# A first unit set up in another order: u loaded between r and w, mask rows in another tile, r turned in other banks, a warm-up that multiplies a tile of ones

## The chip, the cores and the metric

The kernel runs on one core of one Trainium2 chip. Its time is the device time of one execution in microseconds (us); each kernel is run several times, and the median is given. A profile is taken of one further execution, with the start and the duration of every instruction of the five engines: TensorE (PE; its weight loads are PEld), VectorE (DVE), ScalarE (ACT), GpSimd (POOL) and SyncE (SP, which here only issues DMAs).

## The reference

A linear attention with a decaying state (rwkv6) is followed by a feed-forward layer with SiLU. All inputs are float32; B, H, S, D are 4, 8, 768, 48.

```python
state = zeros((B, H, D, D))
for t in range(S):
    cur = einsum('bhd,bhe->bhde', u[None] * k[:, :, t], v[:, :, t])
    y[:, :, t] = einsum('bhd,bhde->bhe', r[:, :, t], state + cur)
    state = w[:, :, t, :, None] * state + einsum('bhd,bhe->bhde', k[:, :, t], v[:, :, t])
x = y.transpose(0, 2, 1, 3).reshape(B * S, H * D)      # 3072 x 384
h = x @ w_in                                           # 384 x 2048
out = (h * (1 / (1 + exp(-h)))) @ w_out                # 2048 x 384
```

The term with u, here called the bonus, is what a token gives to itself: the sum over d of r * u * k, times v.

## The kernel before, in words

The work is cut into 12 units: 128 tokens of two of the four batch entries, all eight heads. A unit's scores (token against token, with the product of the decays between them) are built level by level: at level l, blocks of 2^l tokens are joined in pairs. For that the keys of the odd blocks are multiplied by products of the decays (`grow_keys`, L646 on GpSimd) and the queries by others (`grow_queries`, L628 on VectorE), TensorE multiplies them (`score_products`, L704 and L712), and masked copies take the new part over into `score` (`keep_masked`, L722). `start_keys` (L670) is the first step on the keys: two instructions with `own` true, two with `own` false, each over a quarter of the tokens, all with the decays of the odd tokens. `odd_ones` (L660, ScalarE) copies the keys that need no product at level 0 into the rows from which level 1 reads. `product` (L414) makes the pairwise products of the decays for the next level.

The order of every engine's queue is written out by hand: a call records its instructions in the order in which it stands, each engine takes its own in order, and a framework adds the semaphore waits. What follows concerns only the first unit's start.

- **Loads.** `load_tokens(0)` (L114) issues k, r and w as two halves each, one on SP's queue and one on ScalarE's. SP then issues u, spread over the 128 partitions (L281), the first piece of the weight `w_in` (L211), the tokens of unit 1 and further weights.
- **Set-up.** VectorE clears small tiles (L264 to L269). GpSimd makes the identity `ident`, writes rows of token numbers with iota (L330) into the first part of `score`, from which VectorE compares out the masks (L341, L344), and clears `score` when the last mask is made (L346); it then clears `block_sums` (L465).
- **Warm-up.** `beat(n)` (L1374) issues n transposes of `ident` into a PSUM bank that nobody reads. The first `beat`, of 16, stands ahead of the first turn; smaller ones (3, 5, 6, 2, 2) stand between later steps of unit 0.
- **Turns.** `turn(0, b, name)` brings a half of k, r or w, tokens on partitions, into the layout with features on partitions: eight matmuls against `ident` (`turn_in`, L377) into one of the two banks `p_m`, taken alternately, then copies by ScalarE (`turn_out`, L385 and L386 for k, L389 for r and w). The two banks `p_sc` are used later, for scores.
- **Bonus.** `bonus(0, x)` multiplies r and k, token by token and with the neighbour (x = 0 on GpSimd, L440; x = 1 on VectorE, L442), and then by u (x = 2, VectorE, L444). `bonus_sum` adds over the features (L449, L453), `bonus_spread` brings the sums to their tokens with four matmuls (L586), and `bonus_part` writes them into `score` (L602).
- **Order.** The call of `do` at L1384 sets unit 0's sequence up to level 1. In it `odd_ones` stands behind the turns of k, ahead of the turns of r. `bonus(0, 2)`, the product with u, stands behind the first sum and the turns of w.

Of the kernel before, what the change touches and what calls it, by code (L numbers as in the profile page):

```python
# [8 lines left out]
F32 = mybir.dt.float32  # L9
# [29 lines left out]
def kernel(  # L39
# [63 lines left out]
    def twos(room):  # L103

        flat = room.rearrange("p b h d -> p (b h d)")
        return flat[:, 0:H * 2 * D].rearrange("p (h s) -> p h s", h=H), flat[:, H * 2 * D:H * 2 * D + PD - D]
# [7 lines left out]
    def load_tokens(i):  # L114
        for name, src in (("k", k), ("r", r), ("w", w)):
            load_twos(twos(raw[:, i % NSLOT, WRK[name]])[0], src, i, [nc.sync, nc.scalar if i == 0 else nc.sync])
# [144 lines left out]

    load_tokens(0)
    zero = const.tile([128, 1], F32, name="zero")
# [8 lines left out]
    u_bc = const.tile([128, H, D], F32, name="u_bc")  # L272

# [7 lines left out]
    nc.sync.dma_start(out=u_bc, in_=u.partition_broadcast(128))  # L281
# [44 lines left out]
    for l in range(NL):  # L326
        c, ni = 1 << l, L >> (l + 1)

        first[l] = score[:, 0, 0].rearrange("p q t -> p (q t)")[:, l * 64:(l + 1) * 64].rearrange("p (i c) -> p i c", c=c)
        nc.gpsimd.iota(first[l], pattern=[[2 * c, ni], [0, c]], base=0, channel_multiplier=0,  # L330
                       allow_small_or_imprecise_dtypes=True)
        if l > 0:
            if l < NL - 2:
                masks[l] = const.tile([128, NB, ni, c], I8, name=f"mask{l}")
            else:
                masks[l] = late_masks[:, l - NL + 2].rearrange("p b (i c) -> p b i c", c=c)
# [33 lines left out]
    def turn_in(i, s, name):  # L370

        flat = raw[:, i % NSLOT, WRK[name]].rearrange("p b h d -> p (b h d)")
        p_tr = bank("p_m", NP, NB, L // 2)
# [17 lines left out]
    def clear_rest():  # L391

        for i in range(NSLOT):
            nc.gpsimd.memset(raw[:, i].rearrange("p x b h d -> p x (b h d)")[:, :, H * 2 * D + PD - D:], 0.0)
# [70 lines left out]
    nc.gpsimd.memset(block_sums, 0.0)  # L465
# [908 lines left out]
    def beat(n):  # L1374

        p = bank("p_m", L)
        for x in range(n):
            nc.tensor.transpose(p, ident, ident)

    def back(fn, i, *args):  # L1380
# [3 lines left out]
    do((make_spread,), (beat, 16), *both(turn, 0, "k"), (odd_ones, 0), (bonus, 0, 0), (bonus, 0, 1), *both(turn, 0, "r"),  # L1384
       (bonus_sum, 0, 0), (clear_state,), (clear_rest,), *back(turn, 0, "w"), (bonus, 0, 2), (bonus_sum, 0, 1), (start_keys, 0, nc.vector, True),
# [108 lines left out]
```

## Time and profile before

| What | us |
|---|---|
| median of 3 runs | 566.85 |
| lowest, highest | 566.71, 567.15 |
| the profiled execution's own time | 567.41 |
| its span, from first to last instruction | 565.6 |
| VectorE, GpSimd busy | 477.0, 395.7 |
| ScalarE busy | 274.5 |

Rows of the first 15 us, from the timeline (start, length):

| Row | us |
|---|---|
| `ident` ready on GpSimd (masks.py:199) | 1.01, 0.29 |
| `score` cleared by GpSimd (L346) | 5.64, 1.80 |
| product of r and k on VectorE (L442), after a wait for r's transfer | 7.11, 0.96 |
| neighbour product on GpSimd (L440) | 7.56, 1.38 |
| first sum on VectorE (L449) | 8.97, 0.55 |
| product with u on VectorE (L444) | 9.44, 0.95 |
| copies of w on ScalarE (L389) | 10.95, 0.64 and 11.82, 0.64 |
| start_keys on VectorE (L670, four) | 11.62, 1.31 |

How to read it: the chain of work that ended last is followed back from the last instruction, at each step to what released it, or to the instruction before it on its engine. Times count from the first instruction of the span. A matmul's duration covers its way through the array, and the next begins before it has ended, so starts, not durations, give the pace. Shares of busy time are averages over the whole span, and the part that is changed here is its first fortieth.

### The profile page before, as it was taken

Reading aid. Unit: us, or ns where it says so; the run is one execution under the profiler, and the core shown is the slowest. Engines: PE = TensorE matmul, PEld = TensorE weight load, DVE = VectorE, ACT = ScalarE, POOL = GpSimd, SP = SyncE. Lnnn points to the kernel's source line nnn. Section 1 sums busy time; section 2 is a strip of 40 time slices with the busy share of each in tenths; the row PEclk is TensorE's granted clock in tenths of the full one; section 3 lists DMA queues with packets and bytes.
Section 4 is the critical chain, followed back from the end, with each engine's and each line's share of the span. In section 5 each row is a group of like instructions: output and inputs, shape, how many; then the busy total and the mean of one; then the engine's idle time right before and its main releaser. Section 6 shows DMA issues by size and latency. Waiting matters only on the chain.

```text
span 565.6 us, 18886 instructions
## 1 busy us (share of the span) xinstructions
PE 555.8 (98%) x7782; PEld 517.6 (92%) x7782; DVE 477.0 (84%) x744; ACT 274.5 (49%) x620; POOL 395.7 (70%) x447
## 2 busy tenths in 40 slices
PE   8989999999999999999999999999999999999997
PEld 8767786699889999999999999999999999999997
DVE  7979788998999989999889989989989989882250
ACT  5679696362371373373374274274274272371330
POOL 5998988617879998969796696696696696700000
PEclk9999999999999999999999999999999999999999
DMA  9956876345345365365565554555555462102000
GB/s 224 314 104 191 213 213 133 49 69 115 99 76 99 80 105 94 59 131 95 104 104 93 113 93 89 108 96 94 111 88 95 99 102 65 38 5 57 29 9 21
DMA packets 206485, 57.59 MB, mean 102 GB/s; under 512 B 186048, under 2 KB 198208, under 8 KB 206400
## 3 DMA queue, kind: packets, MB, share of 16 engines
q1 hardware_dynamic: 203712, 54.23, 46.9%
q10 hardware_dynamic: 2688, 2.16, 1.6%
q8 instruction: 61, 1.00, 0.8%
q14 instruction: 24, 0.20, 0.1%
HBM read 47.14 MB, written 9.18 MB: 100 GB/s over the span
## 4 chain that ended last, share of the span: by engine, by line
PE 78%; DVE 8%; POOL 7%; DMA 3%; issue 2%; ACT 1%; SPq 0%; POOLq 0%; DVEq 0%
PE p_o L1335 24%; PE p_o L1191 14%; PE p_h L1191 9%; PE p_h L1084 8%; PE p_h L1335 4%; PE p_m L1273 4%; PE p_sc L704 3%; PE p_m L868 2%; PE p_sc L1335 2%; POOL tk L646 2%; POOL w_in_sb L260 2%; PE p_m L847 1%; DVE tr L628 1%; PE p_m L704 1%; POOL tw L414 1%
## 5 line engine op out<-in xcount | busy, mean ns | idle before, releaser
L646 POOL TENSOR_TENSOR tk<-tk,tw 128x256 f32<-128x256 f32 x112 | 91.7, 839 | 7.6 <-DVE tw L414 3.4
L1335 PE MATMUL p_o<-own,temps 128*128 128x192 f32 x496 | 82.9, 326 | 0.0
L1335 PEld LDWEIGHTS p_o<-own,temps 128*128 128x128 f32 x496 | 80.8, 190 | 0.3 <-DVE temps L1306 0.2
L1191 PE MATMUL p_o<-xt,w_in_sb 128*64 128x128 f32 x1152 | 72.5, 273 | 0.1
L414 POOL TENSOR_TENSOR tw<-tw 128x256 f32<-128x256 f32 (+6 forms) x71 | 42.3, 596 | 38.0 <-DVE tw L365 34.5
L1084 PE MATMUL p_h<-xt,w_in_sb 128*128 128x256 f32 x288 | 66.1, 384 | 1.8 <-POOL w_in_sb L260 1.6
L1191 PEld LDWEIGHTS p_o<-xt,w_in_sb 128*64 128x64 f32 x1152 | 64.9, 137 | 0.4 <-issue 0.4
L1084 PEld LDWEIGHTS p_h<-xt,w_in_sb 128*128 128x128 f32 x288 | 53.6, 190 | 10.0 <-POOL w_in_sb L260 2.4
L497 POOL TENSOR_TENSOR ruk<-tokens_rk 128x384 f32<-128x384 f32 x48 | 53.6, 1137 | 8.1 <-DMA tokens_rk<-in_k_dram 8.1
L1335 PE MATMUL p_o<-w_out_sb,gt 128*128 128x192 f32 x308 | 54.5, 330 | 0.4 <-DVE ob L1343 0.3
L628 DVE TENSOR_TENSOR tr<-tr,tw 128x512 f32<-128x512 f32 x57 | 51.9, 911 | 1.0 <-PE p_m L704 0.4
L1335 PEld LDWEIGHTS p_o<-w_out_sb,gt 128*128 128x128 f32 x308 | 50.0, 190 | 1.5 <-DVE ob L1343 0.9
L655 POOL TENSOR_TENSOR tk<-tk,tw 128x256 f32<-128x256 f32 x32 | 25.1, 812 | 27.5 <-DVE tk L365 27.5
L1306 DVE TENSOR_TENSOR temps<-gt 128x512 f32<-128x512 f32 (+1 forms) x48 | 42.9, 931 | 0.0
L1340 ACT COPY partial<-p_o 128x192 f32<-128x192 f32 x31 | 9.9, 319 | 66.6 <-PE p_o L1335 61.5
L616 ACT COPY tk<-tk 128x256 f32<-128x256 f32 x52 | 20.9, 402 | 37.2 <-POOL tk L646 27.4
L1215 ACT ACTIVATE gt<-p_o 128x512 f32<-128x512 f32 x45 | 26.0, 601 | 25.0 <-PE p_o L1191 25.0
L1335 PE MATMUL p_o<-w_out_sb,temps 128*128 128x192 f32 x176 | 30.5, 326 | 0.0
L722 DVE COPY_PREDICATED score<-mask,p_sc 128x512 f32<-128x512 int8 x38 | 28.4, 807 | 1.4 <-PE p_sc L704 1.3
L1335 PE MATMUL p_h<-w_out_sb,gt 128*128 128x192 f32 x168 | 29.1, 326 | 0.0
L1335 PEld LDWEIGHTS p_o<-w_out_sb,temps 128*128 128x128 f32 x176 | 28.9, 190 | 0.1
L497 POOL TENSOR_TENSOR spare<-tokens_rk 128x384 f32<-128x384 f32 x24 | 28.5, 1198 | 0.6
(251 smaller groups left out, 1314.0 us busy)
## 6 DMA issues: line engine op xcount, KB each, us to landing
w_out_sb<-in_moe_w_in_dram SPq DMA_DIRECT2D x6, 768.0 KB, 7.4
turned<-yt SPq DMA_DIRECT2D x18, 192.0 KB, 2.7
xt<-turned SPq DMA_DIRECT2D x9, 384.0 KB, 3.3
w_out_sb<-in_moe_w_out_dram SPq DMA_DIRECT2D x4, 768.0 KB, 7.4
own<-in_moe_w_out_dram SPq DMA_DIRECT2D x4, 768.0 KB, 4.7
tokens_w<-in_w_dram SPq DMA_DIRECT2D x8, 384.0 KB, 4.5
tokens_rk<-in_r_dram SPq DMA_DIRECT2D x7, 384.0 KB, 4.4
tokens_rk<-in_k_dram SPq DMA_DIRECT2D x7, 384.0 KB, 5.8
```

What stands on the lines that cost most here:

```text
L414: engine.tensor_tensor(out=up, in0=t[:, :, 0::2], in1=t[:, :, 1::2], op=ALU.mult)
L497: mul = lambda out, one, two: nc.gpsimd.tensor_tensor(out=out, in0=one, in1=two, op=ALU.mult)
L628: nc.vector.tensor_tensor(out=odd, in0=odd, in1=tw[i][l][:, :, 0::2][:, :, :, None].to_broadcast([128, Q, L >> (l + 1), c]), op=ALU.mult)
L646: nc.gpsimd.tensor_tensor(out=out, in0=have, in1=odd_products(i, l, b, *blocks), op=ALU.mult)
L655: nc.gpsimd.tensor_tensor(out=have, in0=have, in1=odd_products(i, l, b, [2, NP * ni]), op=ALU.mult)
L704: nc.tensor.matmul(to, lhsT=tk[i][rows, X[l % 2] + p, x * 64:(x + 1) * 64], rhs=have, start=True, stop=True)
L722: nc.vector.copy_predicated(out=dst, mask=masks[l][:, :, None].to_broadcast([128, NB, NP, ni, c]), data=sc[e].rearrange("p (b q) (i c) -> ...
L1084: nc.tensor.matmul(p_h[:, a, :], lhsT=w_in_sb[:, c, f * 128:(f + 1) * 128], rhs=xt[i][:, c, :], start=(a == 0 and c == 0), stop=(a == 1 an ...
L1191: nc.tensor.matmul(p[h:h + PD, q, :], lhsT=left[:, f:f + PD], rhs=right, start=first and q == 0, stop=q == 3, skip_group_check=True)
L1215: nc.scalar.activation(out=g(f, t), in_=have, func=AF.Silu)
L1306: nc.vector.tensor_tensor(out=out, in0=one, in1=two, op=op)
L1335: nc.tensor.matmul(p, lhsT=left(f), rhs=right[:, f, :], start=which in (0, 1, 3) and f == 0, stop=f == FH - 1, skip_group_check=True)
```

## The change

Only what belongs to the first unit's start is touched.

- u is issued on SP's queue inside `load_tokens(0)`, between r and w, and no longer behind w.
- The rows of token numbers are written into the third part of `temps`, not into `score`.
- The turns of r of unit 0 go into the banks `p_sc`, not `p_m`.
- The first `beat` has 17 in place of 16, and it works on `heat`, a 128x128 piece of `w_in_sb` that VectorE sets to 1.0 as its first instruction. All beats are now plain matmuls and not transposes; the later ones still work on `ident`.
- `odd_ones` stands behind the turns of w, `bonus(0, 2)` behind the turns of r and ahead of the first sum.
- GpSimd clears `block_sums` in `clear_rest`, behind the neighbour product and `state`.

```diff
     def load_tokens(i):
         for name, src in (("k", k), ("r", r), ("w", w)):
+            if i == 0 and name == "w":
+                nc.sync.dma_start(out=u_bc, in_=u.partition_broadcast(128))
             load_twos(...)
...
+    u_bc = const.tile([128, H, D], F32, name="u_bc")
     load_tokens(0)
+    heat = w_in_sb[:, 0, 0:128]
+    nc.vector.memset(heat, 1.0)
...
-    u_bc = const.tile([128, H, D], F32, name="u_bc")
...
-    nc.sync.dma_start(out=u_bc, in_=u.partition_broadcast(128))
     load_weight(0)
...
-        first[l] = score[:, 0, 0].rearrange("p q t -> p (q t)")[:, l * 64:(l + 1) * 64].rearrange("p (i c) -> p i c", c=c)
+        first[l] = temps[:, 2, 0].bitcast(F32)[:, l * 64:(l + 1) * 64].rearrange("p (i c) -> p i c", c=c)
...
-        p_tr = bank("p_m", NP, NB, L // 2)
+        p_tr = bank("p_sc" if (i, name) == (0, "r") else "p_m", NP, NB, L // 2)
...
     def clear_rest():
+        nc.gpsimd.memset(block_sums, 0.0)
...
-    nc.gpsimd.memset(block_sums, 0.0)
...
-    def beat(n):
+    def beat(n, have=None):
+        have = ident if have is None else have
         p = bank("p_m", L)
         for x in range(n):
-            nc.tensor.transpose(p, ident, ident)
+            nc.tensor.matmul(p, lhsT=have, rhs=have, start=True, stop=True)
...
-    do((make_spread,), (beat, 16), *both(turn, 0, "k"), (odd_ones, 0), (bonus, 0, 0), (bonus, 0, 1), *both(turn, 0, "r"),
-       (bonus_sum, 0, 0), (clear_state,), (clear_rest,), *back(turn, 0, "w"), (bonus, 0, 2), (bonus_sum, 0, 1), (start_keys, 0, nc.vector, True),
+    do((make_spread,), (beat, 17, heat), *both(turn, 0, "k"), (bonus, 0, 0), (bonus, 0, 1), *both(turn, 0, "r"),
+       (bonus, 0, 2), (bonus_sum, 0, 0), (clear_state,), (clear_rest,), *back(turn, 0, "w"), (odd_ones, 0), (bonus_sum, 0, 1), (start_keys, 0, nc.vector, True),
        (start_keys, 0, nc.vector, False), (grow_queries, 0, 0), (product, 0, 0, nc.vector), (odd_keys, 0, 1), (grow_keys, 0, 1),
        (beat, 3), (bonus_spread, 0), (beat, 5), (bonus_part, 0))
```

## The prediction

> **What bounds the kernel now.** The page first, then the chain of work that ended last in its first 18 us (start, length, what), then the timelines of the engines there. The page's first part:
>
> ```profile
> PE 555.8 (98%) x7782; PEld 517.6 (92%) x7782; DVE 477.0 (84%) x744; ACT 274.5 (49%) x620; POOL 395.7 (70%) x447
> ```
>
> TensorE is busy for 98% of the span, so whatever is late at the start of the first unit moves the whole rest of the kernel: nothing behind it has room to catch up. The change lies in the first 14 us, so the chain there decides:
>
> ```profile
> 1.36 3.67 PE p_m L1378 x16
> 5.03 2.78 PE p_m L377 x32
> ...
> 8.54 0.68 ACT tk L660
> 9.23 0.54 ACT tr L389
> ...
> 9.81 1.12 PE p_m L377 x16
> ...
> 10.95 0.65 ACT tw L389
> ...
> 11.62 1.31 DVE tk L670 x4
> 12.93 0.60 DVE tr L628
> 13.53 0.61 DVE tw L414
> ...
> 14.27 1.89 POOL tk L646 x2
> ```
>
> The reader is to see an unbroken ladder: warm-up, turn k (with ScalarE's copies of k from 7.83 behind it), odd_ones (L660), the copy of r, turn w, copy w, four start_keys on VectorE (L670), grow_queries (L628), product (L414), and then GpSimd. My yardstick is the start of L628, 12.83 by its own row; what it is late, the kernel is late.
>
> The timeline of TensorE gives the price of a matmul (xN counts rows of the trace), and the view by source line its durations (minimum, median, maximum ns; first and last start):
>
> ```profile
> 1.36 3.67 PE L1378 MATMUL p_m<-ident 128*128 128x128 f32 x16 [1.36 <-POOL ident masks.py:199]
> ...
> 12.09 0.96 PE L586 MATMUL p_w<-own_sums,partial 128*128 128x16 f32 x8
> ...
> 23.40 0.91 PE L403 MATMUL p_m<-vq,partial 128*128 128x384 f32 x2
> ```
>
> ```profile
> L1378 PE MATMUL p_m<-ident x16: 421/421/474, 1.4 to 4.6; 128*128 128x128 f32 x16
> ...
> L377 PE MATMUL p_m<-ident,raw x21: 272/273/421, 6.3 to 7.7; 128*64 128x128 f32 x21
> ```
>
> Sixteen transposes of beat leave 16 rows. The one plain f32 matmul of reverse_v (L403) leaves two, the four of bonus_spread (L586) eight. So a plain f32 matmul is two passes through the array and a transpose is one; the page's 7782 is the same count (194 transposes, and twice the 3794 plain matmuls that the program issues).
>
> A pass of 128 columns starts 0.213 us after the one before in the warm-up ((3.67 - 0.42) / 15 = 0.217, of which the first alone takes more) and, later, about 0.11 (L586: (0.96 - 0.26) / 7 = 0.10; the six beats at 14.69: (0.87 - 0.27) / 5 = 0.12). The durations fall from 421 to 273 ns at about 6.5: TensorE's clock rises there, 5.16 us after the first beat, although the windows view prints a granted clock of 1.00 for 1.36 to 5.00 too.
>
> **The change part by part.** Sums are made against the profiled execution (span 565.6, time 567.41, which is 0.56 above the median of the runs).
>
> *Warm-up.* The first beat no longer waits for ident (1.30) but for a 128x128 memset, the first on VectorE. Its first memset began at 0.80; a 128x16 one there takes 0.07, GpSimd's 128x128 one 0.20, so it ends between 0.87 and 1.00. I take 1.00 and the same 0.05 to TensorE: 1.05, 0.3 earlier. But 17 plain matmuls are 34 passes where 16 were. With the clock rising 5.16 after the first beat, at 6.21, they cost 24 x 0.213 = 5.1 and 10 x 0.11 = 1.1: the last ends at **7.27**. The turns of k cannot overtake it on TensorE's queue; before they began at 5.00, just behind the landing of k. This is the costly part, and no other work covers it.
>
> *Turns.* With r in p_sc, nothing in k, r or w waits for odd_ones or for the copies of r any more. Six groups follow at the fast clock, 0.88 each: the two copies of w began 0.87 apart (10.95, 11.82). w begins at 7.27 + 4 x 0.88 = 10.8; its copy came 1.14 behind it (9.81, 10.95): 11.95, ending 12.59 (0.64); the second copy begins at 12.82. The landings are off the path: r is there at 7.0 (VectorE's L442 waits for it until 7.11), w before 9.81.
>
> *u between r and w.* Moved ahead of w's first half on SP's queue, so that half is issued 0.64 later (u's issue time), the weights after it unchanged. In both orders the same bytes have landed by 9.4, when L444 had read u; w is first needed at 10.8. Cost 0, hidden behind the warm-up; without that cover at most 0.64.
>
> *odd_ones behind the copies of w.* On ScalarE it now starts about 0.6 after the second copy of w (the two copies of r were 0.6 apart), at 13.4, and takes 0.68: 14.1. The built program makes the third start_keys instruction wait for it; before all four waited for the first copy of w alone. Queued behind it on VectorE are the fourth, L628 and L414, for which GpSimd waits. So L670 goes on at 14.13, L628 follows two steps of 0.30 later, at **14.73**. By the old order it would be 12.59 + 1.24 = 13.83: of the loss, 0.9 is this wait.
>
> *Bonus on VectorE, GpSimd's order, masks.* The product with u is put ahead of the first sum: VectorE has 7.11 + 0.96 + 0.95 + 3 x 0.53 = 10.6 as its end, 11.4 at worst if u came as late as 9.4, against 11.43 before. The masks' rows in temps let GpSimd clear score at 3.8, not 5.64; its chain then ends before 11.4 in either order, and it is next needed at 14.2. All cost 0, hidden behind the copy of w (12.59).
>
> *The later beats.* They double as well: 3 + 5 (8 more passes, 0.88), 6 (0.66), 2 and 2 (0.22 each). The first two: TensorE is free of w at 12.6, waits for the copy to 12.7, then 6 x 0.11 + 0.81 + 0.1 + 10 x 0.11 = 15.4; scores wait for L628 until 14.73 + 0.70 = 15.43. The six: 15.43 + 1.0 + 1.3 = 17.8, against GpSimd's grow_keys at 14.73 + 0.6 + 0.84 + 1.9 = 18.1. The pairs stand in waits for VectorE of some 0.3. All hidden, by 0.1 to 0.3; uncovered, 0.9 at most.
>
> Sum: 14.73 - 12.83 = **+1.9 us**. The profiled execution would become 569.3, the median 568.7.
>
> *The clock.* Its rise is the one large unknown: the trace has a single one. The row: 5.16 us after the first transpose, 1.52 after the first plain matmul (5.00). If the first interval holds, 6.21; if it keeps its place in the program, 6.52, which gives 7.4 and +2.1. Bounds from rows: 1.05 + 1.52 = 2.57 at the early end, and not within the beats at the late end (34 x 0.213: 8.3, +2.9). [...]
>
> **The rivals.**
>
> *The clock rises early* (2.57, 1.52 after the first plain matmul): 7 passes at 0.213 and 27 at 0.11 end at 5.5. Then k is done by 7.3, when r is there; w begins at 9.0, its second copy at 11.0, odd_ones ends at 12.3, L628 starts at 12.9: **+0.1**, 566.9. [...] Against it: those 1.52 us are a short time next to 5.16 of steady transposes. [...]
>
> *A beat stays one pass*, not slower: 17 passes end before k lands, k begins at 4.97, w at 9.1 (behind r's landing), the second copy at 11.1, odd_ones ends at 12.4, L628 at 13.0: **+0.2**, 567.0. The reordering's own 0.7 (the first copy of w ends at 10.9, not 11.59) is eaten by the wait for odd_ones. Against it: no plain f32 matmul in the trace leaves one row.
>
> *Faster, the change does what it says:* the place is the third start_keys; if its wait for ScalarE did not bind (odd_ones done by 11.5) and the beats ended by 5.3, L628 would start at 10.9 + 1.24 = 12.14: **-0.7**, 566.15. It decides from a warm-up end of 5.3 downwards. Against it: the wait stands in the program, and odd_ones stands behind both copies of w.
>
> *The clock rises only after the beats*: +2.9, 569.7.
>
> **How the numbers follow.** A change under 0.2% (1.13 us) cannot be told from none here. Forecast (+1.1 to +2.5, rise between 4.7 and 7.5): 0.69. Late clock: 0.08. Early clock, +0.1 to +1.1: 0.13. One pass: 0.06. Faster cases: 0.04, some of them within 0.2%. That gives slower 0.76, same 0.21, faster 0.03. The time is the forecast's, 568.7. The range reaches down into the early clock and up to most of the late one: 567.0 to 569.5 leaves out some 0.08 below and 0.08 above.
>
> **What would show it.** In the profile after: 34 rows of the first beat, ending near 7.3, the first turn of k right behind; the matmul durations falling from 421 to 273 ns inside the beats; odd_ones last of ScalarE's five copies; a gap of 0.8 or so between the second and the third L670, ended by odd_ones; L628 near 14.7; GpSimd's first grow_keys near 16.1, not 14.27. Wrong would be 17 rows in the first beat, a clock that rises before 4, no gap in start_keys, or a later part of the chain that takes back what the start lost.

## The result and the profile after

The changed kernel takes 569.95 us (median of 6 runs, 569.29 to 570.37), the kernel before, run beside it, 567.15 (566.71 to 567.58). The ratio is 1.0049, with a 95% interval of 1.0036 to 1.0062: **2.8 us slower**. The forecast was +1.9, a time of 568.7 and a range up to 569.5. The direction was right, the time lies above the range. Of the 1.25 us between forecast and time, 0.3 is the kernel before itself, which now has a median of 567.15 and not 566.85; the rest is the change.

The profiled execution after has a time of 569.86 and a span of 568.1 (before 567.41 and 565.6), 2.45 later than the one before. The page's first part, to be laid beside the line that the prediction shows:

```profile
PE 559.5 (98%) x7818; PEld 522.2 (92%) x7818; DVE 481.1 (85%) x745; ACT 275.1 (48%) x620; POOL 396.5 (70%) x447
```

TensorE has 36 rows more: 18 in the first beat (34 for 16) and 18 in the later ones (36 for 18). So a plain matmul of beat leaves two rows, as forecast. The view by source line has their durations:

```profile
L1381 PE MATMUL p_m<-w_in_sb x34: 275/421/582, 1.1 to 7.3; 128*128 128x128 f32 x34
```

They fall from 421 to 275 ns inside the beats; the trace's record of the granted clock has the rise at 6.33, 5.28 after the first beat (5.16 had been assumed from the durations before, where the same record has 5.33). In the kernel after, every line number stands two or three higher: L630 is the old L628, L672 the old L670, L662 odd_ones (old L660), L417 the old L414, L714 the old L712, L379 the turns, L1381 the beats. Now the chain of work that ended last, in its first 20 us (start, length, what):

```profile
1.06 6.55 PE p_m L1381 x34
7.61 1.90 PE p_m L379 x32
...
13.01 0.86 PE p_m L1381 x6
13.87 0.80 PE p_w L588 x8
14.67 1.21 PE p_m L1381 x10
15.88 1.14 PE p_h L714 x16
17.02 1.53 PE p_m L1381 x12
18.56 1.09 PE p_sc L714 x16
```

Compare it with the ladder of before: from the first beat on, no ScalarE, no VectorE and no GpSimd is in it. **TensorE's own queue** is the chain, without a gap. (The chain counts each piece from the end of the one before it; a row's own start in the timeline can be 0.07 earlier. Differences between kernels are taken from the timelines below.) The timeline of VectorE beside it (start, length, what; in brackets the idle time ahead and what ended it) shows that what the prediction had counted on is there too:

```profile
12.84 0.71 DVE L672 TENSOR_TENSOR tk<-tk,tw 128x128 f32<-128x128 f32 x2 [0.40 <-ACT tw L391]
14.40 0.70 DVE L672 TENSOR_TENSOR tk<-tk,tw 128x128 f32<-128x128 f32 x2 [0.84 <-ACT tk L662]
15.01 0.68 DVE L630 TENSOR_TENSOR tr<-tr,tw 128x512 f32<-128x512 f32 x1
```

The gap of 0.84 between the second and the third start_keys is there, ended by odd_ones, and grow_queries (L630) starts at 15.01, against 14.73 forecast. But it ends at 15.7, and TensorE comes to the scores (L714) only at 15.84: the gap is hidden.

To see where TensorE's queue came from, its timeline in the kernel before, and then in the kernel after:

```profile
11.71 0.55 PE L1378 MATMUL p_m<-ident 128*128 128x128 f32 x3
...
13.58 1.18 PE L712 MATMUL p_h<-tr,tk 48*128 48x128 f32 x16
...
16.21 1.16 PE L712 MATMUL p_sc<-tr,tk 48*128 48x128 f32 x16 [0.64 <-POOL tk L646]
...
21.28 1.16 PE L712 MATMUL p_sc<-tr,tk 48*128 48x128 f32 x16
```

```profile
12.94 0.94 PE L1381 MATMUL p_m<-ident 128*128 128x128 f32 x6
...
15.84 1.18 PE L714 MATMUL p_h<-tr,tk 48*128 48x128 f32 x16
...
18.49 1.16 PE L714 MATMUL p_sc<-tr,tk 48*128 48x128 f32 x16
...
24.00 1.16 PE L714 MATMUL p_sc<-tr,tk 48*128 48x128 f32 x16
```

Behind the last turn of w the later beats begin at 11.71 before and 12.94 after: +1.23. From there to the first scores TensorE needs 13.58 - 11.71 = 1.87 before and 15.84 - 12.94 = 2.90 after: +1.03, eight more passes of the later beats with 0.12 each. Together that is the lateness of the first scores, 2.26. Before, TensorE then stood idle for 0.64 in front of the second scores; after, its six beats (twelve passes) last until them, and they are 2.28 late. From the second scores to the fourth, with the two pairs of beats between them, it needs 5.07 before and 5.51 after: +0.44.

**A yardstick.** A difference in this start is the same for a long time after. The 32 rows of scores that begin at 103.73 in the kernel before show it well:

```profile
103.73 0.69 PE L704 MATMUL p_sc<-tr,tk 48*64 48x64 f32 x32
```

```profile
106.38 0.69 PE L706 MATMUL p_sc<-tr,tk 48*64 48x64 f32 x32
```

The changed kernel is 2.65 late here. Between 150 and 310 us the two executions then shift against one another, to 2.48 at the end; in other kernels' profiles this later part gave -0.54 to +1.12. The change doesn't touch that part, and why it shifts was not found. So below, "late" is the lateness of this group of scores: it holds the start alone, and that of one execution. Times are given beside it.

### The profile page after: what moved, and what is told of

Same layout as the page of the kernel before. It is cut to its first block, busy times and chain, and to the rows that moved or that the text cites. A ratio compares the mean times of both kernels' runs of the same rounds, so it can differ in the third digit from the quotient of the medians.

```text
span 568.1 us, 18958 instructions
## 1 busy us (share of the span) xinstructions
PE 559.5 (98%) x7818; PEld 522.2 (92%) x7818; DVE 481.1 (85%) x745; ACT 275.1 (48%) x620; POOL 396.5 (70%) x447
## 4 chain that ended last, share of the span: by engine, by line
PE 87%; DVE 6%; POOL 3%; issue 2%; SPq 1%; DMA 0%; ACT 0%; DVEq 0%; POOLq 0%
PE p_o L1337 26%; PE p_o L1193 15%; PE p_h L1193 11%; PE p_h L1086 7%; PE p_h L1337 5%; PE p_m L1275 4%; PE p_sc L706 3%; PE p_m L870 2%; PE p_m L1381 2%; PE p_sc L1337 2%; POOL w_in_sb L262 2%; PE p_m L849 2%; PE p_m L706 2%; PE p_m L379 2%; DVE temps L1308 1%
## 5 line engine op out<-in xcount | busy, mean ns | idle before, releaser
L417 POOL TENSOR_TENSOR tw<-tw 128x256 f32<-128x256 f32 (+6 forms) x71 | 42.9, 604 | 37.4 <-DVE tw L367 34.0
L630 DVE TENSOR_TENSOR tr<-tr,tw 128x512 f32<-128x512 f32 x57 | 51.3, 900 | 1.4 <-PE p_m L706 0.4
```

What stands on the lines that cost most here:

```text
L417: engine.tensor_tensor(out=up, in0=t[:, :, 0::2], in1=t[:, :, 1::2], op=ALU.mult)
L630: nc.vector.tensor_tensor(out=odd, in0=odd, in1=tw[i][l][:, :, 0::2][:, :, :, None].to_broadcast([128, Q, L >> (l + 1), c]), op=ALU.mult)
```

## The experiments

Each kernel ran 5 to 12 times beside the kernel before, whose median was 567.00 to 567.29 in these groups; the ratio is to its own group. "k begins" is the start of the first turn of k on TensorE, "late" is the yardstick, both from the one profiled execution. A dash stands where TensorE's clock fell to half again in that execution between 14 and 28 us (the last section), so that the yardstick says nothing of the edit.

| kernel | median, us | ratio to before, 95% | k begins | late |
|---|---|---|---|---|
| before | 567.15 | 1 | 5.00 | 0 |
| after | 569.95 | 1.0049 [1.0036, 1.0062] | 7.54 | 2.65 |
| beats_only | 570.41 | 1.0051 [1.0039, 1.0063] | 7.21 | 2.95 |
| order_only | 569.17 | 1.0054 [1.0031, 1.0078] | 5.33 | 1.92 |
| u_only | 567.98 | 1.0020 [1.0011, 1.0030] | 5.06 | 0.85 |
| masks_only | 568.48 | 1.0021 [1.0004, 1.0038] | 5.06 | - |
| warm_eight | 570.09 | 1.0049 [1.0037, 1.0061] | 5.04 | 2.02 |
| u_back | 569.24 | 1.0035 [1.0023, 1.0047] | 6.98 | 2.07 |
| masks_back | 569.53 | 1.0041 [1.0027, 1.0055] | 7.26 | 2.34 |
| late_transposes | 569.79 | 1.0050 [1.0031, 1.0070] | 7.70 | - |
| odd_early | 570.21 | 1.0049 [1.0034, 1.0063] | 7.67 | 3.06 |
| half_beats | 570.13 | 1.0056 [1.0038, 1.0074] | 7.57 | 2.28 |
| half_odd | 569.43 | 1.0043 [1.0031, 1.0056] | 7.12 | 0.88 |
| warm_u | 569.80 | 1.0042 [1.0028, 1.0056] | 5.00 | 2.24 |
| warm_u_odd | 569.88 | 1.0037 [1.0016, 1.0057] | 5.26 | 1.16 |
| mended | 566.80 | 0.9996 [0.9988, 1.0005] | 4.96 | 0.53 |
| mended_17 | 568.12 | 1.0013 [1.0002, 1.0024] | 6.89 | 0.59 |
| mended_plain | 568.48 | 1.0021 [1.0012, 1.0031] | 5.18 | 0.31 |
| mended_masks | 567.84 | 1.0017 [1.0000, 1.0034] | 5.10 | - |
| mended_odd | 569.12 | 1.0045 [1.0023, 1.0068] | 5.15 | -0.12 |

### Beats or order: each alone

beats_only is the kernel before with the new beats, `heat` included, and nothing else:

```diff
-            nc.tensor.transpose(p, ident, ident)
+            nc.tensor.matmul(p, lhsT=have, rhs=have, start=True, stop=True)
...
-    do((make_spread,), (beat, 16), *both(turn, 0, "k"), (odd_ones, 0), (bonus, 0, 0), (bonus, 0, 1), *both(turn, 0, "r"),
+    do((make_spread,), (beat, 17, heat), *both(turn, 0, "k"), (odd_ones, 0), (bonus, 0, 0), (bonus, 0, 1), *both(turn, 0, "r"),
```


> The kernel before, with the beats of the change alone: 17 plain matmuls of a tile of ones first, plain matmuls of ident later, odd_ones and all else as before. If the passes carry the loss, the first beat leaves 34 rows and ends near 7.5, ScalarE's copy of w ends near 13.5, grow_queries (L628) starts near 14.7 instead of 12.83, the later beats add 0.4: +2.3 us over before. If the wait of start_keys for odd_ones were half of the loss, as the prediction had it, +1.2 to +1.4, since odd_ones stands early here. If the new order (u, masks, banks) made the loss, about 0.

order_only is the changed kernel with the beats of before, against it:

```diff
-            nc.tensor.matmul(p, lhsT=have, rhs=have, start=True, stop=True)
+            nc.tensor.transpose(p, ident, ident)
...
-    do((make_spread,), (beat, 17, heat), *both(turn, 0, "k"), (bonus, 0, 0), (bonus, 0, 1), *both(turn, 0, "r"),
+    do((make_spread,), (beat, 16), *both(turn, 0, "k"), (bonus, 0, 0), (bonus, 0, 1), *both(turn, 0, "r"),
```


> The changed kernel with the beats of before (16 transposes of ident first, transposes later): the new order alone. By the prediction's sum for a short warm-up: +0.2 us (L628's counterpart at 13.0, after odd_ones at 12.4). By what the profile after shows of VectorE (its masks wait behind GpSimd's memsets and its bonus ends at 12.44): start_keys go on at 12.5, grow_queries at about 13.7, +0.9 us. If the order does what it says: -0.7 us.

Measured: +2.9 us for the beats by the ratio, +3.1 for the order; 2.95 and 1.92 late. The ratio of the order is too high for the start: in three of its eight executions the mean granted clock was 0.991 or less (571.64 to 573.91 us), and the other five have a median of 568.92, +1.8. So the beats alone cost as much as both (2.65), and the order alone about three quarters of it; together they would make 4.87. The parts cover one another, and a loss cannot be shared out by adding up. In beats_only the turns end 1.45 late (13.16 for 11.71), and the scores of the yardstick are 2.95 late: beyond the warm-up, the later beats take the other 1.50. In order_only, where none of the three expectations fits, the loss is the old chain with two new delays, both as rows: the copies of w come at 11.92 and 12.79 (10.95 and 11.82 before), since w has landed late, and odd_ones holds the third start_keys until 14.13; L628 starts at 14.75.

### u and the masks

u_only is the kernel before with u between r and w and nothing else:

```diff
+            if i == 0 and name == "w":
+                nc.sync.dma_start(out=u_bc, in_=u.partition_broadcast(128))
```


> The kernel before with one edit, u issued between r and w. Theory now: u's 128 pieces of 1.5 KB, ahead of w on SP's queue, hold up what lands behind them; in the three profiles with u first, w's half from ScalarE's queue lands at 9.1 to 10.1 instead of 7.9. Then the turns of w start near 10.9 instead of 9.8, grow_queries (L628) near 13.9, and the kernel is 1.0 to 1.6 us slower than before. The prediction's account: u costs 0, at most 0.64 if uncovered, so 0 to 0.6.

u_back is the changed kernel with u behind w again:

```diff
-            if i == 0 and name == "w":
-                nc.sync.dma_start(out=u_bc, in_=u.partition_broadcast(128))
...
+    nc.sync.dma_start(out=u_bc, in_=u.partition_broadcast(128))
```


> The changed kernel with u behind w again. If the 34 passes alone suffice to make w late (the last beat ends at 7.5, w is turned from 11.1, after w has landed in either order), nothing is gained: +2.3 to +2.8 us. If u's place carries the loss by itself, below +1.5 us.

masks_only is the kernel before with this edit alone, masks_back the changed kernel without it:

```diff
-        first[l] = score[:, 0, 0].rearrange("p q t -> p (q t)")[:, l * 64:(l + 1) * 64].rearrange("p (i c) -> p i c", c=c)
+        first[l] = temps[:, 2, 0].bitcast(F32)[:, l * 64:(l + 1) * 64].rearrange("p (i c) -> p i c", c=c)
```


> The kernel before with one edit, the mask rows in temps, so that GpSimd clears score while VectorE still makes masks. The profile after shows the masks waiting out GpSimd's memsets and products (two of them from 6.9 to 10.0) and the bonus sums done at 12.4 instead of 11.4. With the old order of the bonus start_keys would then go on near 12.5 and not 11.6: +0.9 us. The prediction's account: cost 0, hidden behind the copies of w.

> The changed kernel with the mask rows back in score, nothing else. Theory now held: VectorE's comparisons no longer stand beside GpSimd's clearing of score, 0.25 us each and not 0.25 to 2.5; VectorE is done with the bonus by about 11.4 and not 12.44, but the copy of w ends at 12.8 in both: gain 0 to 0.2. Rival, the 0.5 to 1.4 of the masks alone counts here as well: gain 0.5 or more, ratio 1.004 or less.

u alone costs +1.1 by the ratio and 0.85 by the yardstick. The chain of u_only in its first 12 us (SPq is SP's queue, which issues):

```profile
2.46 0.63 SPq L117
...
3.15 7.41 DMA raw<-in_w_dram
...
10.69 1.11 PE p_m L378 x16
```

u is issued (L117) ahead of w's first half, and that half lands 7.41 after its own issue, at 10.55; the turn waits for it. Not the 0.64 of SP's queue counts, then, but the transfer of u itself, 128 copies of a row of 1.5 KB in front of w. The landing of w's other half, on ScalarE's queue, says the same: 5.7 after its issue before, 7.4 here (the view of DMA issues). Over all 20 profiles that half took 6.7 to 8.4 in the nine kernels with u between r and w, and 5.5 to 6.0 in nine of the eleven with u behind w. In the changed kernel the long warm-up hides this: u_back is 2.07 late, 0.58 less than after, but its k begins 0.56 earlier (6.98 for 7.54; the clock rose at 5.13 in that execution, for 6.33). What is left for u is 0.02 by the yardstick. Its ratio is lower by 0.0014, with intervals that overlap, so the times leave more room.

The masks bring something that the prediction did not have: rows of VectorE that take far longer, with no wait for a semaphore in front of them. First VectorE and then GpSimd in the changed kernel, from the timeline:

```profile
5.56 0.40 DVE L346 TENSOR_SCALAR late_masks<-temps 128x64 int8<-128x64 f32 x2
...
6.86 3.17 DVE L346 TENSOR_SCALAR late_masks<-temps 128x64 int8<-128x64 f32 x2
```

```profile
6.83 1.01 POOL L443 TENSOR_TENSOR tokens_rk<-raw 128x384 f32<-128x384 f32 x1 [1.30 <-DMA raw<-in_r_dram]
7.79 0.74 POOL L400 MEMSET state<- 128x768 f32 x1
...
8.61 1.34 POOL L397 MEMSET raw<- 128x720 f32 x2
```

Two comparisons of the same shape take 0.40 with GpSimd at rest (it did nothing for 1.30 ahead of its product at 6.83) and 3.17 beside its product and clearings (6.83 to 9.95). In the kernel before, GpSimd cleared `score` only when the masks were made (5.64), so the two never met. The bonus ends at 12.44 on VectorE, against 10.6 forecast (11.4 at worst). Even so nothing waits for it: the copy of w ends at 12.81. The edit doesn't always bring this: in half_odd (below), with the masks in `temps` too, r landed later, GpSimd's product began at 7.25, when the comparisons were done, and the same two rows at 6.86 took 0.40. masks_back has VectorE free at 11.10, and is 2.34 late with k beginning 0.28 earlier: 0.03 for the masks. Its ratio lies 0.0008 below that of after, inside both intervals. Where the cover is thinner the masks do bind: in masks_only start_keys begin at 11.88, right behind VectorE's sums and 0.26 later than before; in mended_masks (below) the sums end at 12.56 and start_keys follow in the queue at 12.47, while the copy of w came at 9.76.

### The warm-up's length, and the later beats

warm_eight is the changed kernel with 16 passes in the first beat:

```diff
-    do((make_spread,), (beat, 17, heat), *both(turn, 0, "k"), (bonus, 0, 0), (bonus, 0, 1), *both(turn, 0, "r"),
+    do((make_spread,), (beat, 8, heat), *both(turn, 0, "k"), (bonus, 0, 0), (bonus, 0, 1), *both(turn, 0, "r"),
```


> The changed kernel with 8 in place of 17 in the first beat: 16 passes, as before. If passes are what counts, the first beat leaves 16 rows, ends near 4.7, ahead of k's landing, and the kernel comes to about order_only plus 0.4 for the later beats: +0.6 to +1.3 us over before, 1.5 or more faster than the change. If the number of beats does not matter (the loss comes from odd_ones or from the loads), it stays at +2.5 to +2.8.

late_transposes leaves only the first beat plain:

```diff
-            nc.tensor.matmul(p, lhsT=have, rhs=have, start=True, stop=True)
+            if have is ident:
+                nc.tensor.transpose(p, ident, ident)
+            else:
+                nc.tensor.matmul(p, lhsT=have, rhs=have, start=True, stop=True)
```


> The changed kernel with its 17 plain matmuls first, and transposes in the later beats. The prediction held the later beats to be hidden: no difference from the change, +2.5 to +2.8 us. If they are what added 0.4 between 20 and 26 us in the profile after, +2.2 us, and the lateness of VectorE stays at 2.1 to 2.2 from 14 us to the end.

warm_eight begins k 2.5 earlier and is only 0.63 less late; in the times nothing is left of it (570.09). The turns of w now wait for w (0.84 of idle TensorE, until 10.50), which lands behind u, and the copies of w come at 11.63 and 12.50, 0.55 earlier than after. late_transposes gained nothing that the times show. By itself that would acquit the later beats. The next runs show why it doesn't.

### What hides what: odd_ones and the later beats

odd_early is the changed kernel with odd_ones behind the turns of k again:

```diff
-    do((make_spread,), (beat, 17, heat), *both(turn, 0, "k"), (bonus, 0, 0), (bonus, 0, 1), *both(turn, 0, "r"),
-       (bonus, 0, 2), (bonus_sum, 0, 0), (clear_state,), (clear_rest,), *back(turn, 0, "w"), (odd_ones, 0), (bonus_sum, 0, 1), (start_keys, 0, nc.vector, True),
+    do((make_spread,), (beat, 17, heat), *both(turn, 0, "k"), (odd_ones, 0), (bonus, 0, 0), (bonus, 0, 1), *both(turn, 0, "r"),
+       (bonus, 0, 2), (bonus_sum, 0, 0), (clear_state,), (clear_rest,), *back(turn, 0, "w"), (bonus_sum, 0, 1), (start_keys, 0, nc.vector, True),
```


> The changed kernel with odd_ones back behind the turns of k, nothing else. Theory now held: in the changed kernel TensorE's own queue is the chain from 1.06 to 30 us, and the scores at 15.88 follow the ten passes of the second beat, not L628; so the gap of 0.84 between the second and the third start_keys goes, L628 comes at about 14.1 and not 15.01, but the scores still start at 15.9: gain 0 to 0.3, ratio to before 1.0044 to 1.005. The forecast's own sum: L628 sets the end, so 0.9 is gained, ratio 1.0034 or so.

half_beats is the changed kernel with later beats of 1, 3, 3, 1 and 1:

```diff
-       (beat, 3), (bonus_spread, 0), (beat, 5), (bonus_part, 0))
+       (beat, 1), (bonus_spread, 0), (beat, 3), (bonus_part, 0))
...
-    others = {1: [(beat, 6)], 2: [(turn, 1, 0, "r"), (head_weight, 0), (beat, 2), (bonus_part, 1)],
+    others = {1: [(beat, 3)], 2: [(turn, 1, 0, "r"), (head_weight, 0), (beat, 1), (bonus_part, 1)],
```


> The changed kernel with half the later beats (1, 3, 3, 1, 1 plain matmuls for 3, 5, 6, 2, 2), as many passes as the 18 transposes of before. From the end of the last turn of w to the first scores TensorE's own queue took 2.87 in the changed kernel (13.01 to 15.88) and 1.87 before (11.71 to 13.58). Theory, the later beats and the wait for odd_ones cover one another: TensorE comes to the first scores at about 14.9, but the query product ends only at 15.7 behind the gap of start_keys; first scores at 15.7, gain 0.2 there and 0.3 from the pairs further on, ratio to before 1.0038 to 1.0046. Rival, the later beats alone carry the loss behind the turns: gain 1.0 or more, ratio 1.0032 or less.

half_odd makes both edits.

> The same with odd_ones behind the turns of k too. Theory: both covers gone, first scores at about 14.9 and not 15.88, third scores' lateness 0.3 less as well: gain 1.0 to 1.3 on the changed kernel, ratio to before 1.0025 to 1.0033, although odd_ones alone gave nothing. Rival, neither is in the chain: ratio 1.0045 to 1.005 as with odd_ones alone.

odd_early takes the gap out of start_keys. VectorE's timeline and TensorE's part of the chain there:

```profile
13.35 1.30 DVE L672 TENSOR_TENSOR tk<-tk,tw 128x128 f32<-128x128 f32 x4
```

```profile
15.02 1.21 PE p_m L1381 x10
16.23 1.11 PE p_h L714 x16
```

All four start_keys are one row, L630 starts at 14.56, 0.45 earlier, although w landed late in this execution (8.4 after its issue on ScalarE's queue, 7.5 in after), and the first scores wait for TensorE's beats all the same. No gain, in the times or in the yardstick. half_beats takes the beats away instead, down to the 18 passes of before. Its chain:

```profile
13.08 0.64 ACT tw L391
...
13.73 0.66 ACT tk L662
...
14.42 0.70 DVE tk L672 x2
15.12 0.60 DVE tr L630
...
16.46 1.92 POOL tk L648 x2
...
18.43 1.19 PE p_sc L714 x16
```

This is the prediction's chain to the letter: the second copy of w, odd_ones, the third start_keys, grow_queries, product, GpSimd. It ends at the second scores at 18.43, where TensorE's own queue had them at 18.49 in the changed kernel. One had hidden behind the other, by 0.06. What half_beats does win back lies further on: from the second scores to the fourth it needs 5.12, after 5.51, before 5.07. half_odd, without both, has grow_queries at 13.63, right behind the four start_keys. Its start_keys, from VectorE's timeline, and its first and second scores, from TensorE's:

```profile
12.42 1.31 DVE L672 TENSOR_TENSOR tk<-tk,tw 128x128 f32<-128x128 f32 x4 [0.53 <-ACT tw L391]
```

```profile
14.49 1.18 PE L714 MATMUL p_h<-tr,tk 48*128 48x128 f32 x16
...
17.06 1.16 PE L714 MATMUL p_sc<-tr,tk 48*128 48x128 f32 x16 [0.52 <-POOL tk L648]
```

Its yardstick is 0.88. Put right for where k begins, the gains on after are -0.28 (odd_early: 3.06, k 0.13 later, w late), 0.40 (half_beats) and 1.35 (half_odd, 1.77 less 0.42). The times don't bear this out: half_beats has a higher ratio than after (1.0056), half_odd gains only 0.3 by the ratios where 1.0 to 1.3 was expected, and the intervals overlap. Of half_odd's profiled execution it is known that it lost 0.90 between 150 and 310 us; whether the others did is not.

The profiles of the other kernels, taken together, settle what these two leave thin. Take from each the lateness at the end of the turns (where the later beats begin, 11.71 before) and the yardstick; the difference is what was lost between them:

| later beats | odd_ones | lost behind the turns, us | in |
|---|---|---|---|
| plain, all of them | late | 1.34 to 1.42 | after, u_back, masks_back, warm_eight |
| plain, all of them | early | 1.45 to 1.50 | beats_only, odd_early, mended_plain, warm_u_odd |
| transposes, or half of the plain ones | late | 0.94 to 1.03 | order_only, half_beats, mended_odd |
| transposes, or half of the plain ones | early | -0.03 to 0.08 | u_only, half_odd, mended_17 |

Beside a full set of plain beats the place of odd_ones gains nothing, without it about 1.0. Of the kernels with a yardstick only warm_u (1.78, the masks) and mended (0.38, u) stand outside, with waits of their own that are shown below. So the cover is shown by the chains and the yardstick, and not by the times.

### A version that takes the losses back

mended is the changed kernel with four edits undone, all shown above: u behind w (as in u_back), the masks in `score` (masks_back), odd_ones behind the turns of k (odd_early), the later beats as transposes (late_transposes); and its first beat has eight. Kept are the turns of r in `p_sc`, `heat`, the early product with u and the late clearing of `block_sums`. The line of it that no other has:

```diff
-    do((make_spread,), (beat, 17, heat), *both(turn, 0, "k"), (bonus, 0, 0), (bonus, 0, 1), *both(turn, 0, "r"),
+    do((make_spread,), (beat, 8, heat), *both(turn, 0, "k"), (odd_ones, 0), (bonus, 0, 0), (bonus, 0, 1), *both(turn, 0, "r"),
```


> What is left of the change when its three suspected costs are taken out: r turned in p_sc, the product with u ahead of the first sum, block_sums cleared later, a warm-up of 8 plain matmuls (16 passes) on the tile of ones; but u behind w, mask rows in score, odd_ones behind k, later beats transposes. If those three (and the passes) are all of the loss, the copy of w starts near 10.4, VectorE is free by 11.4, grow_queries starts at 12.2 to 12.7: -0.1 to -0.6 us against before. If something else of the new order costs time, +0.5 or more.

Each of the next four puts one thing back into mended: mended_17 the long first beat, mended_plain the plain later beats, mended_masks the masks in `temps`, mended_odd the place of odd_ones behind the turns of w.

```diff
-    do((make_spread,), (beat, 8, heat), *both(turn, 0, "k"), (odd_ones, 0), (bonus, 0, 0), (bonus, 0, 1), *both(turn, 0, "r"),
+    do((make_spread,), (beat, 17, heat), *both(turn, 0, "k"), (odd_ones, 0), (bonus, 0, 0), (bonus, 0, 1), *both(turn, 0, "r"),
```


> The mended kernel with 17 in place of 8 in its first beat: the long warm-up alone, 34 passes. If TensorE's queue carries it, the first beat ends between 6.9 and 7.5 (by when the clock rises), the copy of w starts 4.64 after that, grow_queries 6.5 after that, at 13.4 to 14.0: +0.8 to +1.4 us against before. If the loss of the change comes from its order, no more than the mended kernel, within 0.3 of before.

```diff
-            if have is ident:
-                nc.tensor.transpose(p, ident, ident)
-            else:
-                nc.tensor.matmul(p, lhsT=have, rhs=have, start=True, stop=True)
+            nc.tensor.matmul(p, lhsT=have, rhs=have, start=True, stop=True)
```


> The mended kernel with plain matmuls in its later beats (3, 5, 6, 2, 2). By the profile after, where TensorE lost 0.4 between 20 and 25 us to them: +0.1 to +0.5 us against before, and the lateness of VectorE grows by 0.3 to 0.5 between 14 and 26 us. If they are hidden, as the prediction had it: as the mended kernel, 0 to -0.4. If they hold up the clock in executions in which it would fall otherwise, no run far above the others, and no fall of the clock between 14 and 25 us in the profile.

```diff
-        first[l] = score[:, 0, 0].rearrange("p q t -> p (q t)")[:, l * 64:(l + 1) * 64].rearrange("p (i c) -> p i c", c=c)
+        first[l] = temps[:, 2, 0].bitcast(F32)[:, l * 64:(l + 1) * 64].rearrange("p (i c) -> p i c", c=c)
```


> The mended kernel with the mask rows in temps: GpSimd's memsets run against VectorE's masks. If they block VectorE, its bonus sums end near 12.4 and start_keys wait for them, not for ScalarE: grow_queries at 13.5 to 13.7, +0.6 to +1.0 us against before. If only transfers and TensorE count: as the mended kernel, 0 to -0.4.

```diff
-    do((make_spread,), (beat, 8, heat), *both(turn, 0, "k"), (odd_ones, 0), (bonus, 0, 0), (bonus, 0, 1), *both(turn, 0, "r"),
-       (bonus, 0, 2), (bonus_sum, 0, 0), (clear_state,), (clear_rest,), *back(turn, 0, "w"), (bonus_sum, 0, 1), (start_keys, 0, nc.vector, True),
+    do((make_spread,), (beat, 8, heat), *both(turn, 0, "k"), (bonus, 0, 0), (bonus, 0, 1), *both(turn, 0, "r"),
+       (bonus, 0, 2), (bonus_sum, 0, 0), (clear_state,), (clear_rest,), *back(turn, 0, "w"), (odd_ones, 0), (bonus_sum, 0, 1), (start_keys, 0, nc.vector, True),
```


> The mended kernel with odd_ones behind the copies of w. The prediction's account of this wait: start_keys' third step waits for it and everything behind is 0.9 later: +0.5 to +0.9 us against before. If the wait is covered by something else, as the mended kernel: 0 to -0.4.

warm_u is the changed kernel with the edits of warm_eight and u_back, warm_u_odd has that of odd_early too; from there only the masks are left to mended_plain:

```diff
-    do((make_spread,), (beat, 17, heat), *both(turn, 0, "k"), (bonus, 0, 0), (bonus, 0, 1), *both(turn, 0, "r"),
+    do((make_spread,), (beat, 8, heat), *both(turn, 0, "k"), (bonus, 0, 0), (bonus, 0, 1), *both(turn, 0, "r"),
```

> The changed kernel with eight beats for seventeen and u issued behind w again: the two edits together that gave +0.1 (eight beats alone) and -0.6 (u alone). Theory, two covers of one another: turns of w free at about 9, copies of w 9.8 and 10.7, so the next in line binds, VectorE's late bonus at 12.4 or odd_ones; L628 at 13.4 to 13.8 and not 15.0, gain 0.9 to 1.5, ratio 1.0023 to 1.0034. Rival, they simply add: gain 0.5, ratio 1.004.

> The kernel of eight beats and u behind w, with odd_ones behind the turns of k as well; it differs from the one with plain later beats that gave +1.2 only in the mask rows, which stand in temps. Theory: VectorE, held up in its comparisons, is free for start_keys at about 12.4, so odd_ones' place gains at most 0.3 more, L628 at 13.4 to 13.7, ratio 1.002 to 1.0033. Rival, odd_ones binds behind u and the warm-up: 0.5 to 0.9 more, down to the +1.2 of the kernel with the masks in score, ratio 1.001 to 1.002.

mended takes back the loss and no more: 0.9996 cannot be told from 1. With one thing put back, each kernel is slower than before: by 0.7 with the long warm-up, 1.2 with the plain later beats, 1.0 with the masks (an interval that reaches 1), by the ratios; by 2.6 with odd_ones, though four of its seven runs had a mean granted clock of 0.991 or less, and the other three have a median of 568.41 (+1.1). The place of odd_ones shows in the rows. grow_queries is called L628 here as in the kernel before, though its line differs. In mended_odd the copies of w come at 9.87 and 10.74, the third start_keys waits until 12.09, and L628 starts at 12.70, against 12.21 in mended_plain with nearly the same copies (9.80 and 10.67):

```profile
12.09 0.70 DVE L671 TENSOR_TENSOR tk<-tk,tw 128x128 f32<-128x128 f32 x2 [0.43 <-ACT tk L661]
```

Here the wait delays L628 by 0.5. That is not the +1.1 of its time: in that very execution the start is no later than before (-0.12), and 1.12 were lost behind the yardstick. So the times of mended_odd don't price odd_ones. mended_plain shows the later beats with nothing in front of them, in its chain:

```profile
12.30 1.21 PE p_m L1380 x10
13.51 1.11 PE p_h L713 x16
14.62 1.53 PE p_m L1380 x12
16.16 1.12 PE p_sc L713 x16
```

L628 starts at 12.21, 0.62 earlier than before, and ends at 12.9. By the timelines the later beats begin 1.14 earlier than before (10.57 for 11.71), the first scores 0.14 earlier, the second 0.12 earlier, and the yardstick is 0.31 late: 0.93 of what L628 had won, and 1.45 of what the turns had won, given back to the later beats. In beats_only they took 1.50. The ratio has more (+1.2) than the yardstick. warm_u_odd, 0.29 early at the end of the turns, is 1.16 late in the same way (ratio 1.0037, against 1.0033 at most expected). warm_u did not do what I expected of it (2.24 late, ratio 1.0042, against 1.0034 at most): in its profile w's half on ScalarE's queue landed 8.0 after its issue, although u was behind it on SP's queue, and the masks stood beside GpSimd until 9.9, so that VectorE was free at 13.19. mended's profile, the slowest of its 11 executions, has a late landing too (7.4 for w). There VectorE waited until 9.86 for u, which its early product needs:

```profile
9.86 0.96 DVE L446 TENSOR_TENSOR tokens_rk<-tokens_rk,u_bc 128x768 f32<-128x768 f32 x1 [1.97 <-DMA u_bc<-in_u_dram]
```

start_keys follow VectorE's sums at 12.12, while the copy of w had ended at 11.74. So putting u behind w makes an early landing of w likelier and not sure, and the product with u, which the change put ahead of the first sum, can then bind; what decides the order of the two queues' transfers is open.

## Why the forecast was too low

By the prediction's own steps, against the profiled execution:

- **Two passes for a plain matmul, one for a transpose.** Right: 34 rows and 36.
- **Warm-up, last beat at 7.27.** Right in kind, 0.27 too short: k begins at 7.54. There were 24 slow passes and 10 fast ones, as forecast; the first took 0.37 and not 0.21, and from the last beat to the first turn it was 0.20 and not 0.11. That the count came out is in part luck: over the nine kernels with these 34 passes k begins at 6.89 to 7.70, by when the clock rises (4.97 to 6.67), with 7.26 in the middle. A forecast from the single rise of one trace could have been 0.4 off either way.
- **Turns.** Right: with k 0.27 later, the copies of w come at 12.18 and 13.05, 0.23 after the forecast's. The third group of turns no longer waits for anything, and the 96 rows of the turns take 12.94 - 7.54 = 5.40, where they took 6.71. That is the change's one gain, 1.31, and it is inside the sum.
- **u, cost 0.** Right in this kernel by the yardstick (0.02), for the reason given. The bound for a missing cover was wrong: 0.64 was SP's issue time, and the transfer itself costs 0.85 (u_only).
- **odd_ones.** Right as a wait (0.84 for 0.9, L630 at 15.01 for 14.73, the 0.27 of the warm-up). As a share of the loss it was wrong: take it away alone, and nothing is gained. The path was wrong with it: "what it is late, the kernel is late" was said of L628, and the scores behind it did not wait for it.
- **Bonus and masks, cost 0.** Right in this kernel, with 0.37 of cover and not 2: 12.44 for 10.6. VectorE's long comparisons beside GpSimd (3.17 for 0.40) were not in the sum.
- **The later beats, "All hidden, by 0.1 to 0.3".** This is the step that failed. The prediction laid TensorE's queue beside L628 (15.4 for 15.43) and beside GpSimd (17.8 for 18.1), each with a margin of a tenth or three, and put the pairs of beats into waits of some 0.3. Measured, TensorE was free of w 0.34 later than the 12.6 of the sum and needed 2.90 to the first scores where the sum had 2.8: it came to them at 15.84, behind the end of L630 (15.7), and to the second at 18.49. The margins were gone, and TensorE's queue, not L630 and GpSimd, set the scores. The pairs were not hidden either: they add 0.44 between the second scores and the fourth. The lateness grows from 2.18 at L630 to 2.26 and 2.28 at the first and second scores and 2.65 at the yardstick: 0.47 for a term put at 0, below the bound of 0.9 that stood beside it.

The sum is then 1.90 forecast, 0.28 more at L630, and 0.47: 2.65, as measured. The later part of the execution takes 0.17 back (2.48), and the medians, 2.8 apart, are 0.35 above the two profiled executions. None of the rivals came: no early clock (6.33, which is 5.28 after the first plain matmul where the rival had 1.52), no single pass, a gap in start_keys. In this kernel the loss has two roots, the warm-up (1.23 at the end of the turns) and what is lost behind them, 1.42. Of that, odd_ones alone makes about 1.0 and the later beats alone about 1.45, so either is enough for the first 1.0. This rests on the rows of one execution of each kernel; the times agree for the kernel as a whole, and for mended, and do not show the split.

What stays open: the scatter between 150 and 310 us, the order in which the two queues' transfers land, and the price of the masks in the kernel before beyond the 0.26 at start_keys, since TensorE's clock fell in the profile of masks_only.

## What to carry to other kernels

Before you replace a transpose by a plain float32 matmul in a warm-up, count its passes (here 34 rows for 17 calls, where 16 transposes left 16) at every place where the same helper is called, and lay TensorE's queue as a whole, not only the step you moved, beside the engine it waits for. A margin of a tenth of a microsecond is no cover; carry such a term with its uncovered price. Where undoing one edit gains nothing, undo two: the chain of the kernel with one taken away names the other. A profile is one execution, so look for the same difference in more than one pair of kernels.

## What the runs showed of the hardware

**The clock rose while only transposes had run.** In u_only the beats are 16 transposes, and the only matmuls ahead of the first turn, which begins at 5.06 (view by source line; minimum, median, maximum ns, first and last start):

```profile
L1379 PE MATMUL p_m<-ident x16: 272/417/472, 1.4 to 4.4; 128*128 128x128 f32 x16
```

The shortest is 272 ns, the fast clock's duration: by the trace's record of the granted clock it rose at 4.20, inside the transposes; in order_only and masks_only at 4.83 and 4.43, before k at 5.33 and 5.06. In these three profiles no plain matmul stood ahead of the rise. Over the 19 profiles that record a rise it came 2.8 to 5.8 us after the first beat, with plain matmuls (2.8 to 5.8) as with transposes (2.8 to 5.3). So it varies by 3 us over these executions; what sets it was not shown. A long warm-up scatters with it: with the same 34 passes, k began at 6.89 where the clock rose at 4.97, and at 7.70 where it rose at 6.67.

**The clock fell again in three profiles.** In those of masks_only, late_transposes and mended_masks TensorE fell to half speed (a granted clock of 0.50 from 17 to 21 us in each) from about 14 to 17 us on, for 6.8 to 13.7 us. The windows view of late_transposes (window, its length, then busy time of PE, PEld, DVE, ACT and POOL with their instructions, the granted clock, the share of DMA, GB/s):

```profile
17.00:24.00 7.00, 7.00 (x52) 5.56 (x51) 6.20 (x8) 2.05 (x4) 5.71 (x9) 0.52 0.96 263
```

The granted clock is 0.52 for these 7 us. Of an execution without a profile only the mean granted clock is known, which doesn't say when it fell. All executions taken, it was 0.994 or less in 14 of 56 of order_only, u_only, masks_only, late_transposes, mended_masks and mended_odd, whose later beats are transposes, in none of 22 of mended and mended_17 with the same later beats, in one of 103 of the kernel before, in none of 61 of the kernels with all their later beats plain, and in one of 12 with half of them. The plain later beats, which cost about 0.4 (odd_ones late) to 1.45 us (early) by the yardstick, may buy a steadier clock; but the kernel before, mended and mended_17 have transposes there too, and only one such execution in 125, so the kind of beat alone does not decide it, and the cause was not shown.

**VectorE's comparisons took longer beside GpSimd's rows.** In the changed kernel 0.40 became 3.17 for two comparisons of 128x64 (L346, 5.56 and 6.86) beside GpSimd's product and clearings (6.83 to 9.95); in half_odd, where that work began behind them (7.25), the same two stayed at 0.40. Why, these rows don't show.
